# Spectral filter and gated feed-forward on one core: six batches sum their filter products ahead of a single inverse matmul, and a new calendar places the side work

## The chip, the cores and the metric

The kernel runs on one core of one Trainium2 chip. The metric is the device time of one execution in microseconds (us); lower is better. The times shown are of several executions of the same program; the profile is of one of them.

## The reference

The input x has 8 batches of 3008 rows by 256 columns. Each column of a batch goes through a real Fourier transform along its rows, is multiplied by a complex filter, and is transformed back. The result is normalized row by row and goes through a gated feed-forward layer.

```python
# _attn_ref
X = np.fft.rfft(x, axis=1)                    # x: 8 x 3008 x 256
F = (filt_r + 1j * filt_i)[None, :, :]
y = np.fft.irfft(X * F, n=x.shape[1], axis=1)
# _moe_ref, on y as 24064 x 256
rms = np.sqrt(np.mean(x * x, axis=-1, keepdims=True) + 1e-06)
xn = x / rms * rms_g
g = xn @ w_gate                               # 256 x 1536
silu = g * (1.0 / (1.0 + np.exp(-g)))
val = xn @ w_val
return (silu * val @ w_out).astype(np.float32)
```

## The kernel before

A transform of 3008 points is done as 64 times 47 points, in four matmul steps for each batch. Step A (`a_unit`, psum tile psa, L192) transforms over 64 points; the result goes to DRAM by `z_store` and comes back in another order by `t2_load`. Step B (`b_unit`, psb, L213) transforms over 47 points: of the 128 output partitions, the first 64 hold real parts and the last 64 imaginary parts. VectorE then multiplies the psum tile twice, by the real filter (L230, s1) and by the imaginary filter (L231, s2). The inverse of step B (`bi_unit`, psi, L239) is a sum of two matmuls per column of the grid, `wi[:, k, 0, :]` with s1 and `wi[:, k, 1, :]` with s2; the second table carries the swap of halves and the sign that a complex product needs. One unit handles two of the 32 grid columns, so a batch has 16 units and a unit has four inverse matmuls. ScalarE copies psi out (L244); `g_store` and `t4_load` go through DRAM again. The last step (`n_unit`, psn, L270) is the inverse over 64 points; ScalarE writes the scaled rows y (L275) and their squares sq (L277). `q_unit` sums the squares by eight very narrow matmuls (psq, L284), VectorE adds the epsilon (u, L288), GpSimd takes the power -1/2 (rho, L290), `rho_move` spreads it over partitions by way of DRAM (rb), and `xn_unit` multiplies on GpSimd (xn, L345).

The feed-forward layer is a list of 576 slots: 8 batches, 6 blocks of 512 rows (448 in the sixth), 12 blocks of 128 hidden columns. A slot issues `gv` (two matmuls each into pg and pv, L360; the Silu on ScalarE, L364; the product hh on VectorE, L365), then whatever the calendar `plan` has for the slot, then `down` for the slot two places earlier (four matmuls into po, L376). While the feed-forward layer of one batch runs, the transform of the next runs in its slots. Instructions go to the engines in the order in which they are written; nothing is moved later, and each engine works through its own list in order.

The order of the transform in the calendar, with t = 72 * (b - 1), is: a at t + 0 to 11, b every second slot from t + 16, the inverse three slots after its b, the n pairs from t + 57 every 8 slots, both halves in neighbouring slots. Batch 1 starts later and is packed closer. The first transform, of batch 0, runs before slot 0.

psum has eight banks: two each for pg and pv, two for po, and two named psM, which rotate over psa, psb, psi, psn and psq alike.

Of the kernel before, what the change touches and what calls it, by code (L numbers as in the profile page):

```python
# [38 lines left out]
def _make_tables():  # L39
    n2 = np.arange(N2)  # L40
    wa = np.zeros((P, P))
    wai = np.zeros((P, P))
    for h in range(2):
        for k2 in range(K2):
            c = np.cos(2 * np.pi * ((n2 * k2) % N2) / N2)
            s = np.sin(2 * np.pi * ((n2 * k2) % N2) / N2)
            r = slice(h * 64, h * 64 + 64)
            wa[r, h * 64 + k2] = c
            wai[h * 64 + k2, r] = c * (1.0 if k2 == 0 else 2.0)
            if k2 == 0:  # L50
                alt = 1.0 - 2.0 * (n2 % 2)
                wa[r, h * 64 + 32] = alt
                wai[h * 64 + 32, r] = alt
            else:
                wa[r, h * 64 + 32 + k2] = -s
                wai[h * 64 + 32 + k2, r] = -2.0 * s
    n1 = np.arange(N1)
    wb = np.zeros((KR, K2, P))
    wi = np.zeros((P, 1, 2, P))
    re, im = slice(0, N1), slice(SL, SL + N1)  # L60
    for k2 in range(K2):
        for s in range(48):

            if s < 24:
                k = k2 + 64 * s
                sign, q = 1.0, s
            else:
                j = s - 23
                k = 64 * j - (k2 if k2 else 32)
                sign, q = -1.0, 32 + s - 24  # L70
                if j == 24 and k2:
                    continue
            th = 2 * np.pi * ((n1 * k) % N) / N
            c, sn = np.cos(th), np.sin(th)
            if k == 0 or k == NF - 1:
                sn = np.zeros(N1)
            if k2:
                wb[re, k2, q] = c
                wb[im, k2, q] = sign * sn
                wb[re, k2, HALF + q] = -sn  # L80
                wb[im, k2, HALF + q] = sign * c
            else:
                src = re if s < 24 else im
                wb[src, k2, q] = c
                wb[src, k2, HALF + q] = -sn
                m = 1.0 if k in (0, NF - 1) else 2.0
                z = np.zeros(N1)
                g = (m * c, -m * sn)
                gr, gi = (g, (z, z)) if s < 24 else ((z, z), g)


                for qq, cols in ((re, 0), (im, 1)):
                    wi[q, 0, 0, qq] = (gr, gi)[cols][0]
                    wi[HALF + q, 0, 0, qq] = (gr, gi)[cols][1]
                    wi[q, 0, 1, qq] = (gr, gi)[cols][1]
                    wi[HALF + q, 0, 1, qq] = -(gr, gi)[cols][0]
    f = np.float16
    wi0 = wi[:, 0] * S_INV_B
    return wa.astype(f), (wai * S_INV_A).astype(f), wb.astype(f), wi0.astype(f), np.eye(P).astype(f)
# [3 lines left out]
def kernel(  # L103
# [27 lines left out]
    t1p = ctx.enter_context(tc.tile_pool(name="t1p", bufs=2))  # L131
    t2p = ctx.enter_context(tc.tile_pool(name="t2p", bufs=3))
    sp = ctx.enter_context(tc.tile_pool(name="sp", bufs=3))
    t3p = ctx.enter_context(tc.tile_pool(name="t3p", bufs=3))
    t4p = ctx.enter_context(tc.tile_pool(name="t4p", bufs=4))
    yp = ctx.enter_context(tc.tile_pool(name="yp", bufs=3))
    sqp = ctx.enter_context(tc.tile_pool(name="sqp", bufs=2))
# [5 lines left out]
    psG = ctx.enter_context(tc.tile_pool(name="psG", bufs=2, space=bass.MemoryType.PSUM))  # L143
    psV = ctx.enter_context(tc.tile_pool(name="psV", bufs=2, space=bass.MemoryType.PSUM))
    psO = ctx.enter_context(tc.tile_pool(name="psO", bufs=1, space=bass.MemoryType.PSUM))
    psM = ctx.enter_context(tc.tile_pool(name="psM", bufs=2, space=bass.MemoryType.PSUM))

    wa = glob.tile([P, P], FP16)
    wai = glob.tile([P, P], FP16)
# [28 lines left out]

    def bank(i, name):

        pool, tag = ((psM, "mx"), (psG, "pg"), (psV, "pv"))[i]
        return pool.tile([P, 512], FP32, tag=tag, name=name)

    def a_unit(b, i):
# [22 lines left out]
        st[b]["t2"][c] = t  # L207

    def b_unit(b, i):
        ps = bank(0 if b else i % 2, "psb").rearrange("p (a d) -> p a d", a=2)  # L210
        for u in range(2):
            k = 2 * i + u
            nc.tensor.matmul(ps[:, u, :], wb[:, k, :], st[b]["t2"][k // KC][:, k % KC, :],  # L213
                             start=True, stop=True)
        c, r = divmod(2 * i, KC)
        f1, f2 = fr[c][:, r:r + 2, :], fi[c][:, r:r + 2, :]
        if b:
            s1 = sp.tile([P, 2, D], FP16, tag="s1", name="s1")
            s2 = sp.tile([P, 2, D], FP16, tag="s2", name="s2")
        else:  # L220
            s1 = hp.tile([P, 512], FP16, tag="sg", name="sg").rearrange("p (a d) -> p a d", a=2)
            s2 = hhs[i % 4].rearrange("p (a d) -> p a d", a=2)
        eng = nc.vector
        if b == 0 and i % 2 and i > 4:
            eng = nc.gpsimd
            v = yp.tile([P, 2, 512], FP32, tag="y", name="v")
            v = v[:, 0, :].rearrange("p (a d) -> p a d", a=2)
            nc.scalar.activation(out=v, in_=ps, func=AXT.Copy)
            ps = v
        eng.tensor_tensor(out=s1, in0=ps, in1=f1, op=ALU.mult)  # L230
        eng.tensor_tensor(out=s2, in0=ps, in1=f2, op=ALU.mult)  # L231
        st[b]["s"][i] = (s1, s2)

    def bi_unit(b, i):
        s12 = st[b]["s"].pop(i)
        ps = bank(0 if b else 2, "psi").rearrange("p (a d) -> p a d", a=2)
        for u in range(2):
            for q in range(2):
                nc.tensor.matmul(ps[:, u, :], wi[:, 2 * i + u, q, :], s12[q][:, u, :],  # L239
                                 start=(q == 0), stop=(q == 1))  # L240
        c, r = divmod(i, 2)
        if r == 0:
            st[b]["t3"][c] = t3p.tile([KR, 4, D], FP16, tag="t3", name="t3")
        nc.scalar.activation(out=st[b]["t3"][c][:, 2 * r:2 * r + 2, :], in_=ps[0:KR], func=AXT.Copy)  # L244
# [18 lines left out]
    def n_unit(b, m, dh):  # L263
        if dh == 0:
            st[b]["y"][m] = yp.tile([P, 2, 512], FP32, tag="y", name="y")
        y = st[b]["y"][m]
        ps = psM.tile([P, 512], FP32, tag="mx", name="psn")
        for q in range(4):
            n1p = 4 * m + q
            nc.tensor.matmul(ps[:, ts(q, P)],  # L270
# [2 lines left out]
        if dh == 0:  # L273
            st[b]["sq"][m] = sqp.tile([P, 2, 512], FP16, tag="sq", name="sq")
        nc.scalar.activation(out=y[:, dh, :], in_=ps, func=AXT.Identity,  # L275
                             scale=gsb[:, dh:dh + 1])
        nc.scalar.activation(out=st[b]["sq"][m][:, dh, :], in_=ps, func=AXT.Square)  # L277

    def q_unit(b, m):
        sq = st[b]["sq"].pop(m)  # L280
        ps = psM.tile([P, 4], FP32, tag="mx", name="psq")
        for q in range(4):
            for dh in range(2):
                nc.tensor.matmul(ps[:, q:q + 1], sq[:, dh, ts(q, P)], ones,  # L284
# [7 lines left out]

    def rho_move(b, m):
        nc.sync.dma_start(r_d[b, m], st[b]["u"].pop(m))
        rb = rp.tile([P, P, 4], FP32, tag="rb", name="rb")
        nc.sync.dma_start(rb.rearrange("p a q -> p (a q)"),
                          r_d[b, m].rearrange("p q -> (p q)").partition_broadcast(P))
# [116 lines left out]

    def f_dup(c):
        nc.vector.tensor_copy(out=fr[c][HALF:P], in_=fr[c][0:HALF])
        nc.scalar.activation(out=fi[c][HALF:P], in_=fi[c][0:HALF], func=AXT.Copy)

    def wi_group(g):

# [3 lines left out]
            nc.tensor.matmul(ps[:, a, :], wb[:, 4 * g + a, :], ident[0:KR, :], start=True, stop=True)  # L424
        k = slice(4 * g + lo, 4 * g + 4)
        nc.scalar.activation(out=wi[:, k, 0, :], in_=ps[:, lo:4, :], func=AXT.Copy, scale=S_INV_B)
        for p0, sign in ((0, 1.0), (HALF, -1.0)):
            nc.vector.tensor_scalar(out=wi[p0:p0 + HALF, k, 1, :],
                                    in0=ps[HALF - p0:P - p0, lo:4, :], scalar1=sign * S_INV_B,
                                    scalar2=None, op0=ALU.mult)  # L430

    def gate(ap):
# [14 lines left out]
    with tc.manual_schedule():  # L447
# [58 lines left out]
        norm_first()  # L506
        w_load(1)
        w_load(2)
        n_unit(0, 1, 0)
        n_unit(0, 1, 1)  # L510
        for c in range(NXC):
            x_load(1, c)

# [1 line left out]
        plan = {}  # L515

        def at(slot, fn, *a):
            plan.setdefault(slot, []).append((fn, a))

        def norm_plan(b, m, s0):  # L520
            at(s0, n_unit, b, m, 0)
            at(s0 + 1, n_unit, b, m, 1)
            at(s0 + 3, q_unit, b, m)
            at(s0 + 5, rho_move, b, m)
            at(s0 + 10, xn_unit, b, m)

        at(1, q_unit, 0, 1)
        at(3, scale_split, 1)
        at(5, scale_apply, 1, 0)
        for m in range(2, 6):  # L530
            norm_plan(0, m, 2 + (m - 2) * 9)
        for b in range(1, B):
            t = (b - 1) * 72
            a0, b0, bs = (8, 24, 6) if b == 1 else (0, 16, 8)
            for i in range(12):
                at(t + a0 + i, a_unit, b, i)
                if i % 3 == 2:
                    at(t + a0 + i + 1, z_store, b, i // 3)
            for c in range(4):
                at(t + b0 - 3 + c if c < 3 else t + b0 + 8, t2_load, b, c)  # L540
            for i in range(16):
                s0 = t + b0 + bs * i // 4
                at(s0, b_unit, b, i)
                at(s0 + 3, bi_unit, b, i)
                if i % 2 == 1:
                    at(s0 + 4, g_store, b, i // 2)
            if b + 1 < B:
                for c in range(NXC):
                    at(t + 20 + 4 * c, x_load, b + 1, c)
            for c in range(4):  # L550
                at(t + 54, t4_load, b, c)
            for m in range(6):
                norm_plan(b, m, t + 57 + 8 * m)

        stores = {}
        for i in range(len(items) + 4):
# [40 lines left out]
```

## Time and profile before

| | |
|---|---|
| median of 8 runs | 991.09 us (988.02 to 994.0) |
| profiled execution: its time | 993.59 us |
| profiled execution: span of its instructions | 991.8 us |
| mean granted TensorE clock | 0.963 |
| TensorE busy | 911.2 us, 92% of the span |
| ScalarE busy | 606.3 us, 61% |
| VectorE busy | 594.1 us, 60% |
| GpSimd busy | 256.2 us, 26% |
| inverse matmuls of step B (psi) | 512, of which 384 belong to batches 2 to 7 |

Busy time is the time in which at least one instruction of the engine was under way. Matmuls overlap each other, so the length of one row is not what the matmul costs; the distance from its start to the start of the next one is. An engine's idle time matters where that engine, or what waits for it, ends last.

### The profile page before, as it was taken

To read this page: it belongs to the slowest core of one execution; us is meant where nothing else is said; L and a number is where in the kernel's file an instruction comes from. 1 tells how busy PE (TensorE), PEld (TensorE's weight loads), DVE (VectorE), ACT (ScalarE), POOL (GpSimd) and SP (SyncE) were. 2 spreads that over 40 slices of the span, in tenths; PEclk is the share of its full clock that TensorE was granted. 3 is DMA by queue.
4 is the path that set the end of the run, shared out by engine and by line. 5 is a ranking of instruction groups with operands and counts; after the bars stand their busy time and mean duration, and the time that the engine had idled before them with its cause. 6 is when DMAs were issued, how large, how long until landed. Compare 5 with 4: busy or idle time off the path is not lost.

```text
span 991.8 us, 17348 instructions
## 1 busy us (share of the span) xinstructions
PE 911.2 (92%) x6287; PEld 576.5 (58%) x6287; DVE 594.1 (60%) x961; ACT 606.3 (61%) x1061; POOL 256.2 (26%) x219
## 2 busy tenths in 40 slices
PE   3347989999999999999999999999999989999997
PEld 1224546665666566665666566665666556666654
DVE  6623468545775467655775468655775467655554
ACT  7343845576656865577656865577656756566543
POOL 3564231033301332032411323031411312024300
PEclk8567999999999999999999999999999999999999
DMA  8879473335623474324814375324734343322211
GB/s 191 141 138 168 111 155 79 106 99 116 152 75 97 104 174 98 102 78 125 163 51 126 88 154 125 108 63 110 164 81 125 88 111 90 99 70 62 43 43 40
DMA packets 94837, 106.98 MB, mean 108 GB/s; under 512 B 17112, under 2 KB 69464, under 8 KB 94560
## 3 DMA queue, kind: packets, MB, share of 16 engines
q1 hardware_dynamic: 85104, 87.92, 34.0%
q0 software_dynamic: 9552, 17.77, 12.0%
q8 instruction: 49, 0.80, 0.3%
q14 instruction: 36, 0.29, 0.1%
q10 hardware_dynamic: 96, 0.20, 0.1%
HBM read 70.62 MB, written 49.90 MB: 122 GB/s over the span
## 4 chain that ended last, share of the span: by engine, by line
PE 76%; DMA 9%; ACT 5%; issue 4%; DVE 3%; POOL 1%; SPq 1%; ACTq 0%; DVEq 0%; POOLq 0%
PE po L376 22%; PE pg L360 21%; PE pv L360 21%; PE psi L239 5%; DMA t<-z_tmp 3%; PE psb L213 3%; DMA fi<-in_filt_i_dram 2%; PE psn L270 2%; DMA g_tmp<-t 1%; DMA z_tmp<-t 1%; PE psa L192 1%; ACT sq L277 1%; ACT t L194 1%; DVE o L382 1%; DMA xc<-in_x_dram 1%
## 5 line engine op out<-in xcount | busy, mean ns | idle before, releaser
L365 DVE TENSOR_TENSOR hh<-pv,sg 128x512 f16<-128x512 f32 (+1 forms) x576 | 390.9, 679 | 333.0 <-ACT sg L364 210.5
L364 ACT ACTIVATE sg<-pg 128x512 f16<-128x512 f32 (+1 forms) x576 | 341.0, 592 | 295.8 <-PE pg L360 271.3
L376 PE MATMUL po<-wo,hh 128*128 128x256 f16 x2304 | 350.8, 273 | 3.5 <-DVE o L382 0.9
L360 PE MATMUL pg<-xn,wg 128*128 128x512 f16 (+1 forms) x1152 | 340.0, 377 | 0.0
L360 PE MATMUL pv<-xn,wv 128*128 128x512 f16 (+1 forms) x1152 | 339.8, 377 | 0.0
L376 PEld LDWEIGHTS <-hh 128*128 128x128 f16 x2304 | 221.3, 98 | 94.6 <-issue 16.4
L345 POOL TENSOR_TENSOR xn<-y,rb 128x1024 f16<-128x1024 f32 x46 | 132.1, 2873 | 315.5 <-DMA rb<-r_tmp 244.1
L360 PEld LDWEIGHTS <-wv 128*128 128x128 f16 x1152 | 113.2, 98 | 132.6 <-issue 3.0
L290 POOL TENSOR_TENSOR rho<-u,mhalf 128x4 f32<-128x4 f32 x48 | 48.7, 1014 | 328.9 <-DVE u L288 328.8
L360 PEld LDWEIGHTS <-wg 128*128 128x128 f16 x1152 | 113.2, 98 | 14.4 <-issue 0.6
L244 ACT ACTIVATE t<-psi 96x512 f16<-96x512 f32 x128 | 75.6, 593 | 32.3 <-PE psi L239 29.3
L239 PEld LDWEIGHTS <-wi 128*128 128x128 f16 x512 | 51.2, 102 | 55.7 <-issue 13.4
L230 DVE TENSOR_TENSOR s<-psb,fr 128x512 f16<-128x512 f32 x112 | 76.4, 682 | 10.0 <-PE psb L213 10.0
L231 DVE TENSOR_TENSOR s<-psb,fi 128x512 f16<-128x512 f32 x112 | 76.3, 681 | 0.0
L275 ACT ACTIVATE y<-psn,gsb 128x512 f32<-128x512 f32 x94 | 65.3, 695 | 10.2 <-PE psn L270 4.9
L213 PE MATMUL psb<-t,wb 96*128 96x256 f16 x256 | 52.4, 290 | 19.4 <-DMA t<-z_tmp 18.5
L239 PE MATMUL psi<-s,wi 128*128 128x256 f16 x448 | 67.3, 273 | 2.6 <-DVE s L231 2.6
L194 ACT ACTIVATE t<-psa 128x512 f16<-128x512 f32 x96 | 57.9, 615 | 5.7 <-PE psa L192 2.8
L277 ACT ACTIVATE sq<-psn 128x512 f16<-128x512 f32 x94 | 56.6, 603 | 0.0
L213 PEld LDWEIGHTS <-wb 96*128 96x128 f16 x256 | 25.1, 104 | 41.1 <-issue 18.3
L192 PE MATMUL psa<-xc,wa 128*128 128x512 f16 x96 | 37.2, 404 | 11.3 <-DMA xc<-in_x_dram 8.9
L270 PEld LDWEIGHTS <-t 128*128 128x128 f16 x376 | 29.4, 99 | 21.3 <-issue 0.6
(55 smaller groups left out, 329.8 us busy)
## 6 DMA issues: line engine op xcount, KB each, us to landing
out_dram<-o SPq DMA_DIRECT2D x88, 256.0 KB, 3.7
z_tmp<-t SPq DMA_DIRECT2D x128, 96.0 KB, 2.2
t<-z_tmp SPq DMA_DIRECT2D x32, 384.0 KB, 6.1
g_tmp<-t SPq DMA_DIRECT2D x64, 192.0 KB, 2.5
t<-g_tmp SPq DMA_DIRECT2D x126, 96.0 KB, 2.6
rb<-r_tmp SPq DMA_DIRECT2D x46, 256.0 KB, 4.1
xc<-in_x_dram POOLq DMA_DIRECT2D x56, 192.0 KB, 6.1
out_dram<-o SPq DMA_DIRECT2D x8, 192.0 KB, 3.0
```

The source lines that it names most:

```text
L194: nc.scalar.activation(out=dst, in_=src, func=AXT.Copy)
L213: nc.tensor.matmul(ps[:, u, :], wb[:, k, :], st[b]["t2"][k // KC][:, k % KC, :], start=True, stop=True)
L230: eng.tensor_tensor(out=s1, in0=ps, in1=f1, op=ALU.mult)
L231: eng.tensor_tensor(out=s2, in0=ps, in1=f2, op=ALU.mult)
L239: nc.tensor.matmul(ps[:, u, :], wi[:, 2 * i + u, q, :], s12[q][:, u, :], start=(q == 0), stop=(q == 1))
L244: nc.scalar.activation(out=st[b]["t3"][c][:, 2 * r:2 * r + 2, :], in_=ps[0:KR], func=AXT.Copy)
L277: nc.scalar.activation(out=st[b]["sq"][m][:, dh, :], in_=ps, func=AXT.Square)
L345: nc.gpsimd.tensor_tensor(out=xv, in0=yv, in1=rv.unsqueeze(1).to_broadcast([P, 2, 4, P]), op=ALU.mult)
L360: nc.tensor.matmul(ps[:, 0:w], wt[:, dt_, ts(jt, P)], xn[:, dt_, 0:w], start=(dt_ == 0), stop=(dt_ == 1))
L364: nc.scalar.activation(out=sg[:, 0:w], in_=pg[:, 0:w], func=AXT.Silu)
L365: nc.vector.tensor_tensor(out=hh[:, 0:w], in0=pv[:, 0:w], in1=sg[:, 0:w], op=ALU.mult)
L376: nc.tensor.matmul(po[s4 // 2][:, s4 % 2, :], hh[:, ts(s4, P)], wo[:, jt, :], start=(jt == 0 and s4 % 2 == 0), stop=(jt == JT - 1 and s4 % ...
```

## The change

For batches 2 to 7, s2 is formed with its halves exchanged: two VectorE products of 64 partitions each (`swap_unit`), reading one half of the psum tile and writing the other half of s2. GpSimd adds s1 and s2 to one tile s, and `bi_unit` does one matmul a column, with `wi[:, k, 0, :]` alone. The sign moves from the table to the copied half of the imaginary filter (`f_dup`, scale -1). Batches 0 and 1 keep two products and two inverse matmuls; in batch 1 every third unit has its products done on GpSimd, from a copy that ScalarE makes.

The two psM banks become one bank psM (psa, psi, psn) and one bank psB (psb, psq). The squares leave `n_unit` for a function of their own, `sq_unit`, which for batches from 1 on stands one slot later. `rho_move` is split in two, so that the load of rb has its own slot. `sq_unit` (from batch 1 on) and `swap_unit` are put at the head of their slot's list, which is still behind the slot's `gv`.

The calendar is new. For batches 3 to 7 a stands in slots that are 1 modulo 4, b and the inverse of two units earlier in slots 2 modulo 4, the first half product and n in slots 3 modulo 4, the second half product and the squares in slots 0 modulo 4, and q in slots 1 modulo 4. Batch 2 has the same grid for b and a lag of 4 slots from b to the inverse where the later batches have 8; its a steps stand in slots 22 to 44, among batch 1's b and inverse steps.

```diff
-                    wi[HALF + q, 0, 1, qq] = -(gr, gi)[cols][0]
+                    wi[HALF + q, 0, 1, qq] = (gr, gi)[cols][0]
...
+    ssp = ctx.enter_context(tc.tile_pool(name="ssp", bufs=3))
+    t3p = ctx.enter_context(tc.tile_pool(name="t3p", bufs=2))
...
-    psM = ctx.enter_context(tc.tile_pool(name="psM", bufs=2, space=bass.MemoryType.PSUM))
+    psM = ctx.enter_context(tc.tile_pool(name="psM", bufs=1, space=bass.MemoryType.PSUM))
+    psB = ctx.enter_context(tc.tile_pool(name="psB", bufs=1, space=bass.MemoryType.PSUM))
...
-        ps = bank(0 if b else i % 2, "psb").rearrange("p (a d) -> p a d", a=2)
+        ps = bank(3 if b else (0, 1, 3)[i % 3], "psb").rearrange("p (a d) -> p a d", a=2)
...
+            if b > 1:
+                nc.vector.tensor_tensor(out=s1, in0=ps, in1=f1, op=ALU.mult)
+                st[b]["s"][i] = (s1, s2, ps, f2)
+                return
...
-        if b == 0 and i % 2 and i > 4:
+        if (b == 0 and i % 2 and i > 4) or (b == 1 and i % 3 == 1):
...
+    def swap_unit(b, i, h):
+        s1, s2, ps, f2 = st[b]["s"][i]
+        a, e = slice(HALF * h, HALF * h + HALF), slice(HALF - HALF * h, P - HALF * h)
+        nc.vector.tensor_tensor(out=s2[a], in0=ps[e], in1=f2[e], op=ALU.mult)
+        if h:
+            s = ssp.tile([P, 2, D], FP16, tag="s", name="s")
+            nc.gpsimd.tensor_tensor(out=s, in0=s1, in1=s2, op=ALU.add)
+            st[b]["s"][i] = (s,)
...
+        n = len(ss)
         for u in range(2):
-            for q in range(2):
-                nc.tensor.matmul(ps[:, u, :], wi[:, 2 * i + u, q, :], s12[q][:, u, :],
-                                 start=(q == 0), stop=(q == 1))
+            for q in range(n):
+                nc.tensor.matmul(ps[:, u, :], wi[:, 2 * i + u, q, :], ss[q][:, u, :],
+                                 start=(q == 0), stop=(q == n - 1))
...
-        nc.scalar.activation(out=st[b]["sq"][m][:, dh, :], in_=ps, func=AXT.Square)
+        st[b]["sq"][m, dh] = ps
+
+    def sq_unit(b, m, dh):
+        nc.scalar.activation(out=st[b]["sq"][m][:, dh, :], in_=st[b]["sq"].pop((m, dh)),
+                             func=AXT.Square)
...
-        ps = psM.tile([P, 4], FP32, tag="mx", name="psq")
+        ps = psB.tile([P, 4], FP32, tag="mb", name="psq")
...
         def at(slot, fn, *a):
-            plan.setdefault(slot, []).append((fn, a))
+            todo = plan.setdefault(slot, [])
+            if fn in (sq_unit, swap_unit) and a[0]:
+                todo.insert(0, (fn, a))
+            else:
+                todo.append((fn, a))
...
+        def norm_plan(b, m, s0, s1, r):
+            for dh in range(2):
+                at((s0, s1)[dh], n_unit, b, m, dh)
+                at((s0, s1)[dh] + (b > 0), sq_unit, b, m, dh)
+            for d, fn in zip(r, (q_unit, rho_move, rho_load, xn_unit)):
+                at(s1 + d, fn, b, m)
...
         for m in range(2, 6):
-            norm_plan(0, m, 2 + (m - 2) * 9)
+            s0 = (2, 20, 28, 38)[m - 2]
+            norm_plan(0, m, s0, s0 + 2, (2, 3, 5, 8))
...
-            a0, b0, bs = (8, 24, 6) if b == 1 else (0, 16, 8)
+            if b == 1:
+                a_at = [8 + i for i in range(12)]
+                b_at = [24 + 3 * i // 2 for i in range(16)]
+                lag, t4_at, n_at = 3, 53, 55
+            elif b == 2:
+                a_at = [22 + 2 * i for i in range(12)]
+                b_at = [50 + 4 * i for i in range(16)]
+                lag, t4_at, n_at = 4, 118, 123
+            else:
+                a_at = [t - 103 + 12 * (i // 2) + 4 * (i % 2) for i in range(12)]
+                b_at = [t - 26 + 4 * i for i in range(16)]
+                lag, t4_at, n_at = 8, t + 46, t + 51
...
-                at(t + b0 - 3 + c if c < 3 else t + b0 + 8, t2_load, b, c)
+                at(b_at[0] - (4 if b > 2 else 3) + c if c < 3 else b_at[4] + 1, t2_load, b, c)
             for i in range(16):
-                s0 = t + b0 + bs * i // 4
+                s0 = b_at[i]
                 at(s0, b_unit, b, i)
-                at(s0 + 3, bi_unit, b, i)
+                if b > 1:
+                    at(s0 + 1, swap_unit, b, i, 0)
+                    at(s0 + 2, swap_unit, b, i, 1)
+                at(s0 + lag, bi_unit, b, i)
...
-                    at(t + 20 + 4 * c, x_load, b + 1, c)
+                    at(a_at[3 * c + 2] + 2, x_load, b + 1, c)
...
-                at(t + 54, t4_load, b, c)
+                at(t4_at + c, t4_load, b, c)
             for m in range(6):
-                norm_plan(b, m, t + 57 + 8 * m)
+                norm_plan(b, m, n_at + 8 * m, n_at + 8 * m + 4,
+                          (2, 4, 6, 10) if b > 1 else (2, 3, 4, 7))
```

More of the change, by code (lines that the diff above doesn't have):

```diff
@@ L133 @@
     sp = ctx.enter_context(tc.tile_pool(name="sp", bufs=3))
-    t3p = ctx.enter_context(tc.tile_pool(name="t3p", bufs=3))
+    ssp = ctx.enter_context(tc.tile_pool(name="ssp", bufs=3))
+    t3p = ctx.enter_context(tc.tile_pool(name="t3p", bufs=2))
     t4p = ctx.enter_context(tc.tile_pool(name="t4p", bufs=4))
@@ L179, in bank @@
     def bank(i, name):
-        pool, tag = ((psM, "mx"), (psG, "pg"), (psV, "pv"))[i]
+        pool, tag = ((psM, "mx"), (psG, "pg"), (psV, "pv"), (psB, "mb"))[i]
         return pool.tile([P, 512], FP32, tag=tag, name=name)
@@ L232, in b_unit @@
         st[b]["s"][i] = (s1, s2)
+    def swap_unit(b, i, h):
[6 more added lines that the diff above has]
+            st[b]["s"][i] = (s,)
     def bi_unit(b, i):
-        s12 = st[b]["s"].pop(i)
+        ss = st[b]["s"].pop(i)
         ps = bank(0 if b else 2, "psi").rearrange("p (a d) -> p a d", a=2)
+        n = len(ss)
         for u in range(2):
-            for q in range(2):
-                nc.tensor.matmul(ps[:, u, :], wi[:, 2 * i + u, q, :], s12[q][:, u, :],
-                                 start=(q == 0), stop=(q == 1))
+            for q in range(n):
+                nc.tensor.matmul(ps[:, u, :], wi[:, 2 * i + u, q, :], ss[q][:, u, :],
+                                 start=(q == 0), stop=(q == n - 1))
         c, r = divmod(i, 2)
@@ L266, in n_unit @@
         y = st[b]["y"][m]
-        ps = psM.tile([P, 512], FP32, tag="mx", name="psn")
+        ps = bank(0, "psn")
         for q in range(4):
@@ L294, in rho_move, with rho_load @@
         nc.sync.dma_start(r_d[b, m], st[b]["u"].pop(m))
+    def rho_load(b, m):
         rb = rp.tile([P, P, 4], FP32, tag="rb", name="rb")
@@ L416, in f_dup @@
         nc.vector.tensor_copy(out=fr[c][HALF:P], in_=fr[c][0:HALF])
-        nc.scalar.activation(out=fi[c][HALF:P], in_=fi[c][0:HALF], func=AXT.Copy)
+        nc.scalar.activation(out=fi[c][HALF:P], in_=fi[c][0:HALF], func=AXT.Copy, scale=-1.0)
     def wi_group(g):
@@ L426, in wi_group @@
         nc.scalar.activation(out=wi[:, k, 0, :], in_=ps[:, lo:4, :], func=AXT.Copy, scale=S_INV_B)
-        for p0, sign in ((0, 1.0), (HALF, -1.0)):
+        for p0 in (0, HALF):
             nc.vector.tensor_scalar(out=wi[p0:p0 + HALF, k, 1, :],
-                                    in0=ps[HALF - p0:P - p0, lo:4, :], scalar1=sign * S_INV_B,
+                                    in0=ps[HALF - p0:P - p0, lo:4, :], scalar1=S_INV_B,
                                     scalar2=None, op0=ALU.mult)
@@ L508 @@
         w_load(2)
-        n_unit(0, 1, 0)
-        n_unit(0, 1, 1)
+        for dh in range(2):
+            n_unit(0, 1, dh)
+            sq_unit(0, 1, dh)
         for c in range(NXC):
@@ L517, in at @@
         def at(slot, fn, *a):
-            plan.setdefault(slot, []).append((fn, a))
[L520 to L525, printed above, removed]
+            todo = plan.setdefault(slot, [])
[4 more added lines that the diff above has]
+        def norm_plan(b, m, s0, s1, r):
+            for dh in range(2):
+                at((s0, s1)[dh], n_unit, b, m, dh)
+                at((s0, s1)[dh] + (b > 0), sq_unit, b, m, dh)
+            for d, fn in zip(r, (q_unit, rho_move, rho_load, xn_unit)):
+                at(s1 + d, fn, b, m)
         at(1, q_unit, 0, 1)
@@ L535 @@
             for i in range(12):
-                at(t + a0 + i, a_unit, b, i)
+                at(a_at[i], a_unit, b, i)
                 if i % 3 == 2:
-                    at(t + a0 + i + 1, z_store, b, i // 3)
+                    at(a_at[i] + 1, z_store, b, i // 3)
             for c in range(4):
-                at(t + b0 - 3 + c if c < 3 else t + b0 + 8, t2_load, b, c)
+                at(b_at[0] - (4 if b > 2 else 3) + c if c < 3 else b_at[4] + 1, t2_load, b, c)
             for i in range(16):
-                s0 = t + b0 + bs * i // 4
+                s0 = b_at[i]
@@ L543 @@
                 at(s0, b_unit, b, i)
-                at(s0 + 3, bi_unit, b, i)
+                if b > 1:
+                    at(s0 + 1, swap_unit, b, i, 0)
+                    at(s0 + 2, swap_unit, b, i, 1)
+                at(s0 + lag, bi_unit, b, i)
                 if i % 2 == 1:
-                    at(s0 + 4, g_store, b, i // 2)
+                    at(s0 + lag + 1, g_store, b, i // 2)
             if b + 1 < B:
                 for c in range(NXC):
-                    at(t + 20 + 4 * c, x_load, b + 1, c)
+                    at(a_at[3 * c + 2] + 2, x_load, b + 1, c)
```

## Prediction

> **What bounds the kernel now.** I read the page first, then busy time by stretch, then the timeline of TensorE, then the other engines around one slot.
>
> ```profile
> PE   3347989999999999999999999999999989999997
> PEclk8567999999999999999999999999999999999999
> PE 76%; DMA 9%; ACT 5%; issue 4%; DVE 3%; POOL 1%; SPq 1%; ACTq 0%; DVEq 0%; POOLq 0%
> 500.00:525.00 25.00, 25.00 (x169) 16.24 (x167) 18.15 (x29) 14.46 (x25) 0.00 (x0) 1.00 0.33 83
> 550.00:575.00 25.00, 24.53 (x169) 14.53 (x168) 12.16 (x21) 20.44 (x37) 7.75 (x4) 1.00 0.43 112
> ```
>
> From slot 8 on (100 us) TensorE is busy nearly all the time, at full clock, and the chain that ended last lies on it for 76%. VectorE (18.15 us in the busier stretch) and ScalarE (20.44) have room. So matmul columns taken out, and waits of TensorE taken out or put in, are what counts.
>
> ```profile
> 566.39 0.39 PE L270 MATMUL psn<-wai,t 128*128 128x128 f16 x4
> 566.91 0.38 PE L192 MATMUL psa<-xc,wa 128*128 128x512 f16 x1
> 576.67 0.38 PE L213 MATMUL psb<-t,wb 96*128 96x256 f16 x2 [0.92 <-DMA t<-z_tmp]
> ...
> 581.03 0.59 PE L360 MATMUL pv<-xn,wv 128*128 128x512 f16 x2
> 581.46 0.60 PE L239 MATMUL psi<-s,wi 128*128 128x256 f16 x4
> 581.89 0.60 PE L376 MATMUL po<-wo,hh 128*128 128x256 f16 x4
> 582.33 0.59 PE L360 MATMUL pg<-xn,wg 128*128 128x512 f16 x2
> ```
>
> Read from start to start, an inverse unit of four matmuls costs 581.89 - 581.46 = 0.43 us, as po does; pg and pv 0.43 each, so a bare slot is 1.30. Psn, psa or psb cost 0.22, psq 0.20. The first two rows are 0.52 apart, not 0.22: psa waited 0.30 for a psum bank. Slots 72 to 503 (206.9 to 888.4 us) last 681.5 us; subtracting these contents (blocks of 448 rows cost 0.107 a slot less) leaves 25.4 us of waiting, some 3 to 6 a batch: psn and psa in one slot, the first psb behind its load, a VectorE copy of po in front of the products. Before slot 72 the same reading leaves 16.6, after slot 504 2.9.
>
> ```profile
> 478.82 0.39 PE L270 MATMUL psn<-wai,t 128*128 128x128 f16 x4
> 479.31 0.69 ACT L275 ACTIVATE y<-psn,gsb 128x512 f32<-128x512 f32 x1
> 479.89 0.59 ACT L277 ACTIVATE sq<-psn 128x512 f16<-128x512 f32 x1
> 484.01 0.59 PE L360 MATMUL pg<-xn,wg 128*128 128x512 f16 x2
> 484.64 0.60 ACT L364 ACTIVATE sg<-pg 128x512 f16<-128x512 f32 x1 [0.28 <-PE pg L360]
> 485.27 0.69 DVE L365 TENSOR_TENSOR hh<-pv,sg 128x512 f16<-128x512 f32 x1 [0.83 <-ACT sg L364]
> ...
> 22.50 5.63 DVE L428 TENSOR_SCALAR wi<-pst 64x512 f16<-64x512 f32 x8 [3.12 <-ACT wi L426]
> 29.48 0.69 DVE L230 TENSOR_TENSOR sg<-psb,fr 128x512 f16<-128x512 f32 x1 [0.21 <-PE psb L213]
> 30.09 0.68 DVE L231 TENSOR_TENSOR hh<-psb,fi 128x512 f16<-128x512 f32 x1
> L230 POOL TENSOR_TENSOR sg<-v,fr x6: 1252/1259/1280, 44.7 to 64.8; 128x512 f16<-128x512 f32 x6
> ```
>
> These are the clocks of a slot that starts at T: the Silu at T + 0.63, hh at T + 1.26. A psn bank is held from 478.82 to 480.48, 1.66 us. L428 is the nearest row to a half product, 64 partitions crossing halves: eight take 5.63, 0.70 each, where whole products follow each other after 0.60.
>
> **The change, part by part.**
>
> *Matmuls.* 6 batches x 16 units x half of 0.434 = **-20.8 us**, all in slots where TensorE has no slack.
>
> *Old waits, slots 72 to 503.* The calendar parts psn from psa, loads t2 four slots ahead of use instead of three and keeps the po copy (slots 1 modulo 12) away from the first product. I let 1.5 of the 25.4 us stay: **-23.9**. After slot 504, with the n halves apart: **-0.9**.
>
> *Steady ScalarE and psM, batches 3 to 7.* A slot has one extra activation beside the Silu, 0.59 + 0.70 at most, against slots of 1.30 to 1.74. With one bank psM: a starts at T + 0.87, its copy ends near T + 2.0, the inverse comes at T + 1.52 + 0.87 = 2.39; n comes after the inverse's copy with more room; sq runs from T + 1.13 to 1.73 of its slot, a comes at 1.30 + 0.87 = 2.17. Cost 0, covered by gaps of some 0.4 us; without them each would be paid for by TensorE directly, queued behind it po and the next slot.
>
> *VectorE and psB: q.* Nothing else on VectorE is late (4.8 us of work in four slots of 6.1), but psB is now alone. The second half product stands in slot 0 behind hh: hh from 1.26, 0.69 long, then 0.70, so it ends at 2.65 and the bank is free at about 2.70. q asks for the same bank in the next slot after pg and pv, at 1.30 + 0.87 = 2.17. TensorE waits 0.53 with po behind it. Counting the calendar, each of the 36 q of batches 1 to 6 follows such a half product: **+19.1** (15 if the half product starts 0.60 after hh and lasts 0.68; 0 if something delays q anyway).
>
> *GpSimd adds.* No row shows a sum of f16 tiles; the nearest, L230 on GpSimd at the same 128x512, is 1.26 us; half an xn row (2.87 for 1024) gives 1.44. I take 1.26. For batches 3 to 7 it has 8 slots, 12 us: free, even behind an xn and a rho (2.87 + 1.0); the x loads' issues on GpSimd, two of 0.56, fit too. For batch 2 the lag is 4 slots: the sum ends at 2.70 + 1.26 + 0.05 = 4.0 after its slot 0, the inverse comes at 1.30 + 0.87 + slot 1, which is 3.47 bare, 3.69 with a, over 4.1 with q. Four bare ones wait 0.51, six with a 0.29, six with q none: **+3.8** (6 with 1.44). The Trainium skill speaks against such an add (GPSIMD Engine Reference, Performance versus the Vector engine: about 2.6 cycles an element for two inputs, elementwise work belongs on VectorE); its rate gives an estimate of 1.11 us for 512 elements, which would make the term 2.3. I keep the row, which holds the fixed part too.
>
> *Slots 20 to 50.* Batch 2's a now meets batch 1's inverse and batch 0's n on the one psM bank, and here sq is in n's own slot. Slots 28, 30 and 40 have n, inverse, b, a: the inverse waits from 1.09 until 2.58 (bank held 1.66 + release), a another 0.6 for the inverse's copy: 2.1 each. Slot 38 (n, a) 1.5; 34, 36, 45 (inverse, a) and 42 (b behind q's u) 0.63 each; 32 (q behind b) 0.46: **10.8**. Before, slots 30 and 38 lost 1.09 and 0.75, and 12 to 14 0.35. The wait for the first t2 of batch 1 (3.71 us in the timeline, slot 24) is bound by its load; an n/a collision in slot 22 eats 1.5 of it, so about 2.3 remain. In the trace that 3.71 us gap was followed by pg and pv rows of 1.06 us, half clock, which with slots 25 and 26 cost 1.95 more. The Trainium skill (TensorE: Matmul & The Clock Gate, Part 1) has the clock fall after an idle window of about 3.4 us; by it 2.3 us keep the clock and the 1.95 goes, by the row alone it stays. I take half: 3.3 here against 6.0 before. Together 14.1 - 8.2 = **+5.9**.
>
> *DMA and queues.* No transfer is added. SP is the queue to watch: rho_move now waits there for a rho that stands behind an xn on GpSimd, about 3 us, with g_store and o_store behind it. g_store has 16 slots until its buffer is needed; t4 loads stand three slots behind the last g_store and five ahead of n: 0. Without that cover the 2.0 us of rho's landing would show before n. Start-up up to slot 8 waits for weights and for rho(0,1) in GpSimd's list, which is unchanged: 0; the second n(0,1), now waiting 1.7 us for the bank, hides in the wait of slot 5 (5.9 us).
>
> Sum: -20.8 - 23.9 - 0.9 + 19.1 + 3.8 + 5.9 = **-16.8**; the profiled execution's 993.59 becomes 976.8. It lay 2.5 above the median of 991.09, so the forecast is **974 us**, -1.7%.
>
> **The rivals.**
>
> *The q wait is not there* (slot 0 drawn out by something, or psB free sooner): 974 - 19 = 955. For it: a calendar with nothing in conflict would look so. Against it: the arithmetic rests on hh at T + 1.26, seen in every slot.
>
> *Half given back:* the same mechanisms with larger sizes: adds of 1.44, collisions in slots 20 to 50 that also delay xn (y buffers are shared with batch 1's copies), a late rb. Another 8 to 14 us: 982 to 988.
>
> *Slower: the single psM bank.* Place: a, inverse, n, squares of batches 2 to 7, once in every four slots. They have about 0.4 us to spare. If ScalarE ran its copies 0.6 us later than I read, each of 96 groups would lose 0.2 or more; 17 us, 0.18 a group, cancels the gain, and at 0.25 the time is 974 + 24 = 998. For it: with two banks psa already waits when n is in its slot. Against it: those were two n and two a in neighbouring slots.
>
> *It does not do what it says:* "at most one extra operation" fails in batch 1's stage, and is in the forecast as 10.8 us.
>
> **How the numbers follow.** The forecast 0.58 (966 to 981 by the bounds of q, add and clock), no q wait 0.12, half given back 0.16, slower 0.10, and 0.04 that losses just cancel. A measurement here tells 0.3%, about 3 us, from no change. Faster: 0.58 + 0.12 + 0.16 = 0.86; same 0.04; slower 0.10. The range leaves out the slower and the cancelled cases and the lower half of the case without q waits: 956 to 987.
>
> **What would show it.** psi rows fall from 512 to 320. A bare q slot of 1.51 lasts 2.0, with psq waiting on VectorE's half product, some 36 times. psi of batch 2 waits on GpSimd in ten units, later batches never. Slots 28, 30, 40 last over 4 us. Half products 0.68 to 0.70 and adds near 1.26. Steady stretches hold no other wait of TensorE. I am wrong if a stretch from 350 to 850 us shows TensorE waiting for ScalarE on psM, or no wait before psq.

## The result: 8 us instead of 17

The changed kernel takes 982.86 us (median of 11 runs, 980.46 to 986.01) against 991.11 (32 runs): a ratio of 0.9916, 95% interval 0.9901 to 0.9932. Forecast was 974, a gain of 17; measured is a gain of 8.25. The direction was right and the range held the time; the size was off by half. The profiled execution took 985.8 us with a span of 983.7, so the spans fell by 8.1 us, as the medians did.

The page of the changed kernel, the rows of TensorE's load, granted clock and the chain that ended last, and the same two stretches as before:

```profile
PE   3356978999999999999999999999999999999997
PEclk8556999999999999999999999999999999999999
PE 72%; DVE 8%; DMA 7%; issue 5%; ACT 4%; POOL 3%; SPq 0%; DVEq 0%; POOLq 0%; ACTq 0%
```

```profile
500.00:525.00 25.00, 24.87 (x156) 14.98 (x154) 17.60 (x27) 14.68 (x25) 6.54 (x6) 1.00 0.68 148
550.00:575.00 25.00, 24.20 (x180) 15.48 (x179) 19.37 (x33) 18.70 (x32) 13.32 (x11) 1.00 0.41 91
```

TensorE is still the bound, but VectorE has gone from 3% to 8% of the chain: something on VectorE now ends a wait of TensorE. No stretch looks overloaded; VectorE's 19.37 of 25 us would never suggest it. The waits of TensorE name it. First the kernel before, slots 72 to 503, then the changed kernel, the same slots (us in total, times, longest):

```profile
PE psb L213 <- DMA t<-z_tmp: 9.0, 6, 2.8
```

```profile
PE psq L304 <- DVE s L243: 13.8, 34, 0.4
PE psi L255 <- POOL s L246: 1.9, 5, 0.5
```

The wait for step B's loads is gone. In its place stand 34 waits of psq for the half product (two more stand before slot 72, 36 in all), and some of the inverse for the GpSimd sum. The view counts an idle stretch from the modelled end of the last row, so it shows 0.4 us of each; from start to start it is 0.57. One of them, in the timeline of the changed kernel (start, length):

```profile
572.33 0.69 DVE L243 TENSOR_TENSOR s<-psb,fi 64x512 f16<-64x512 f32 x1
573.13 0.69 DVE L387 TENSOR_TENSOR hh<-pv,sg 128x512 f16<-128x512 f32 x1
573.60 0.59 PE L382 MATMUL pv<-xn,wv 128*128 128x512 f16 x2
573.85 0.68 DVE L243 TENSOR_TENSOR s<-psb,fi 64x512 f16<-64x512 f32 x1
574.60 0.35 PE L304 MATMUL psq<-ones,sq 128*128 128x1 f16 x8 [0.40 <-DVE s L243]
574.71 1.15 POOL L246 TENSOR_TENSOR s<-s,s 128x512 f16<-128x512 f16 x1 [4.92 <-DVE s L243]
```

pv is through at 574.03 (573.60 + 0.43) and psq is next in TensorE's list. The second half product ends at 574.53, psq starts at 574.60. This is the wait that the forecast drew, at the place it named; it cost 0.57 instead of 0.53.

### The profile page after: what moved, and what is told of

Its sections match the earlier page's. It is cut to its first block, busy times and chain, and to the rows that moved or that the text cites. A ratio compares the mean times of both kernels' runs of the same rounds, so it can differ in the third digit from the quotient of the medians.

```text
span 983.7 us, 17361 instructions
## 1 busy us (share of the span) xinstructions
PE 894.0 (91%) x6095; PEld 554.4 (56%) x6095; DVE 670.5 (68%) x1047; ACT 633.5 (64%) x1066; POOL 376.9 (38%) x325
## 4 chain that ended last, share of the span: by engine, by line
PE 72%; DVE 8%; DMA 7%; issue 5%; ACT 4%; POOL 3%; SPq 0%; DVEq 0%; POOLq 0%; ACTq 0%
PE po L398 22%; PE pg L382 21%; PE pv L382 19%; DVE hh L387 4%; DVE s L243 3%; PE psi L255 3%; ACT sg L386 3%; PE psb L215 2%; PE psn L286 2%; PE psa L194 2%; DMA fi<-in_filt_i_dram 2%; DMA g_tmp<-t 2%; PE psq L304 1%; DMA z_tmp<-t 1%; DVE o L404 1%
## 5 line engine op out<-in xcount | busy, mean ns | idle before, releaser
L246 POOL TENSOR_TENSOR s<-s,s 128x512 f16<-128x512 f16 x96 | 110.6, 1152 | 375.4 <-DVE s L243 338.5
L243 DVE TENSOR_TENSOR s<-psb,fi 64x512 f16<-64x512 f32 x192 | 132.2, 689 | 5.9
L255 PEld LDWEIGHTS <-wi 128*128 128x128 f16 x320 | 33.5, 106 | 59.7 <-issue 25.4
L223 DVE TENSOR_TENSOR s<-psb,fr 128x512 f16<-128x512 f32 x96 | 65.5, 682 | 0.7 <-PE psb L215 0.2
L255 PE MATMUL psi<-s,wi 128*128 128x256 f16 x256 | 46.7, 275 | 6.9 <-ACT sq L296 3.9
```

The costliest lines, as they stand in the source:

```text
L223: nc.vector.tensor_tensor(out=s1, in0=ps, in1=f1, op=ALU.mult)
L243: nc.vector.tensor_tensor(out=s2[a], in0=ps[e], in1=f2[e], op=ALU.mult)
L246: nc.gpsimd.tensor_tensor(out=s, in0=s1, in1=s2, op=ALU.add)
L255: nc.tensor.matmul(ps[:, u, :], wi[:, 2 * i + u, q, :], ss[q][:, u, :], start=(q == 0), stop=(q == n - 1))
```

## The experiments

All medians in this section are compared within one session, with its own runs of the kernel before: 994.39 in the first four, 991.2 in the next four, 989.39 in the last two. Lost time in a slot is always read from start to start of TensorE's rows, less 0.217 us for each matmul of 512 columns and in proportion.

**The changed kernel again.** No edit.

> The changed kernel as it is, for comparison on the same chip and to see which waits come back in a second profile. Theory A (all waits follow from the calendar): 983 us, 36 waits of 0.57 us before psq, 2.1 us lost in slots 28, 30 and 40, the pair of half-clock rows near slot 31 again, and about 2 us in slot 18. Theory B (slots 18 and 31 are accidents of one execution): the same time within 3 us, but those two waits are gone or elsewhere.

981.71 us, a ratio of 0.9871 (0.9847 to 0.9894). The 36 psq waits and the losses of slots 28, 30 and 40 (2.13, 2.05, 2.05) are the same to 0.1 us; slot 18 lost 1.7. The half-clock rows of slot 31 (1.6 us in the first profile) are not there. So theory A holds for all but the clock, which differs between executions. The two sessions' ratios differ by more than their intervals allow, mainly through the kernel before; I use the sessions' own references.

**psq behind po.** `q_unit` of batches 1 to 7 is called after `down` in its slot.

```diff
+            late = []
             for fn, a in plan.get(i, ()):
-                fn(*a)
+                if fn is q_unit and a[0]:
+                    late.append(a)
+                else:
+                    fn(*a)
...
+            for a in late:
+                q_unit(*a)
```

> The eight narrow psq matmuls of batches 1 to 7 are issued behind the slot's four po matmuls instead of in front of them; nothing else changes. Theory A (psq waits 0.57 us for the bank that the second half product still reads, 36 times): po fills 0.43 us of that wait, a psa another 0.22, so the time falls by 17 to 20 us, to about 964. Theory B (the wait only moves, to the next slot's b or to po for want of hh): it falls by less than 6 us.

969.82 us, 11.9 less than the changed kernel (0.9751, 0.9726 to 0.9775, against 0.9871). A slot with a step A, in its timeline:

```profile
563.34 0.69 DVE L243 TENSOR_TENSOR s<-psb,fi 64x512 f16<-64x512 f32 x1
563.52 0.38 PE L194 MATMUL psa<-xc,wa 128*128 128x512 f16 x1
563.74 0.60 PE L398 MATMUL po<-wo,hh 128*128 128x256 f16 x4
564.17 0.34 PE L304 MATMUL psq<-ones,sq 128*128 128x1 f16 x8
```

psa follows pv at once, po follows psa, and psq finds the bank free. Of 20.7 us lost in front of psq 2.2 remain; some 2 come back at batch 2's inverse, which a late psq had covered, and 1.2 at the next slot's psb, which now waits 0.12 ten times. The profiled spans of this run and of the changed kernel's second profile differ by 14.7, the medians by 11.9, both short of the 17 to 20 that theory A named. Its cause holds (the bank, and what can stand in front of psq), its size does not; the move takes nothing from po, which does not need what psq needs.

**Other banks in slots 22 to 49.** Batch 2's step A takes its psum from the pv banks, batch 1's inverse from the pg banks.

```diff
-        ps = bank(0 if b else i % 3, "psa")
+        ps = bank((2 if b == 2 else 0) if b else i % 3, "psa")
...
-        ps = bank(0 if b else 2, "psi")
+        ps = bank((1 if b == 1 else 0) if b else 2, "psi")
```

> Step A of batch 2 takes its psum tile from the pv banks and the inverse of batch 1 from the pg banks, so that in slots 22 to 49 only n uses psM. Theory A (the waits of slots 22 to 45 are collisions on the single psM bank): slots 28, 30 and 40 fall from 4.5 to about 2.4 us and slots 34, 36, 45 lose their 0.63; 8 to 11 us less, and with them the half clock of slot 31. Slot 22 gives its 1.4 us to the wait for the load in slot 24. Theory B (ScalarE, with up to four activations in such a slot, is the limit there): pg and pv now wait for the copies instead, and under 4 us are won.

974.86 us, 6.9 less (0.9804, 0.9777 to 0.9832). Slots 28 to 49 lose 2.1 us instead of 10.6 to 12.1. The timelines of slot 30 in the changed kernel and of slot 28 here:

```profile
144.15 0.39 PE L286 MATMUL psn<-wai,t 128*128 128x128 f16 x4
145.16 0.59 ACT L296 ACTIVATE sq<-psn 128x512 f16<-128x512 f32 x1
145.80 0.60 PE L255 MATMUL psi<-s,wi 128*128 128x256 f16 x4 [1.26 <-ACT sq L296]
147.08 0.38 PE L194 MATMUL psa<-xc,wa 128*128 128x512 f16 x1 [0.46 <-ACT t L260]
```

```profile
137.03 0.39 PE L286 MATMUL psn<-wai,t 128*128 128x128 f16 x4
137.26 0.60 PE L255 MATMUL psi<-s,wi 128*128 128x256 f16 x4
137.69 0.38 PE L215 MATMUL psb<-t,wb 96*128 96x256 f16 x2
137.92 0.38 PE L194 MATMUL psa<-xc,wa 128*128 128x512 f16 x1
```

Above, the inverse starts 1.65 us after psn because one bank is read by y and sq first; below, 0.23 after. ScalarE has the same activations and is not the limit. Slots 18 to 20 lost 2 us more than in the changed kernel in this profile, 1.7 of it in rows at half clock behind the wait of slot 18, so not all of the 8.5 to 10 us arrived; the medians' 6.9 lies under the 8 to 11 of theory A, whose cause the timeline shows.

**Two products and two inverse matmuls, new calendar.** The half products and the sum are left out.

```diff
-        nc.vector.tensor_tensor(out=s2[a], in0=ps[e], in1=f2[e], op=ALU.mult)
-        if h:
-            s = ssp.tile([P, 2, D], FP16, tag="s", name="s")
-            nc.gpsimd.tensor_tensor(out=s, in0=s1, in1=s2, op=ALU.add)
-            st[b]["s"][i] = (s,)
+        nc.vector.tensor_tensor(out=s2, in0=ps, in1=f2, op=ALU.mult)
+        st[b]["s"][i] = (s1, s2)
...
-                    at(s0 + 2, swap_unit, b, i, 1)
```

> The calendar, banks and lags of the changed kernel, but batches 2 to 7 form two whole products as before (the second one a slot after the first), no sum, and two inverse matmuls a column. It puts back 20.8 us of matmul and takes away the GpSimd sums and one of three VectorE operations. Theory A (the sum's gain was eaten by the waits that it brought: psB held a slot longer in front of q, 20.7 us, and batch 2's inverse behind the sum, 4.7 us): 983 + 20.8 - 25.4 = 978, no slower than the changed kernel, with no wait before psq. Theory B (q waits for another reason, the calendar's): 983 + 20.8 = 1004, q waits stay.

973.91 us, 7.8 less than the changed kernel although it does all the matmuls of the kernel before (0.9802, 0.9775 to 0.9829). In slots 72 to 503 TensorE waits for next to nothing: 0.8 us by the starts. Its page:

```profile
PE 900.0 (93%) x6287; PEld 574.3 (59%) x6287; DVE 594.9 (61%) x951; ACT 633.2 (65%) x1066; POOL 269.1 (28%) x229
PE 85%; DMA 8%; ACT 2%; issue 2%; DVE 1%; POOL 1%; SPq 0%; DVEq 0%; ACTq 0%; POOLq 0%
```

The second product is done one slot after b, so psB is free before psq asks. This is the verdict on the change: **the calendar, with its two single banks and batch 1's products on GpSimd, is worth some 20 us without the sum (2.0%), and the sum, which takes 20.8 us of matmul away, cost 8 on top of it**. The changed kernel loses what this one does not: 20.7 us before psq, 4.7 at batch 2's inverse and some 3 where po waits for the copy of its second bank, 28 in all.

**Later slots for batch 2's x loads.**

```diff
-                    at(a_at[3 * c + 2] + 2, x_load, b + 1, c)
+                    at((18, 23, 29, 35)[c] if b == 1 else a_at[3 * c + 2] + 2, x_load, b + 1, c)
```

> The changed kernel with the four loads of batch 2's x at slots 18, 23, 29 and 35 instead of 12, 15, 18 and 21; step A of batch 2 still starts in slot 22. Theory A (these loads, pulled forward by the new calendar, slow the landing of batch 1's z stores, whose median there rose from 2.7 to 4.2 us and whose longest from 3.4 to 7.5, so that a step A buffer comes free late in slot 18): the 1.7 to 2.1 us of slot 18 go and slot 24 waits less; 2 to 4 us less in all. Theory B (the stores land late for another reason, such as the weights still arriving): slot 18 keeps its wait. A risk: x(2,0) could arrive late for slot 22.

981.11 us (0.9903, 0.9884 to 0.9921); slot 18 still lost 1.95. But the edit had moved only half of what it meant to. Each load is two transfers; the four of the first two loads went out together as in the changed kernel, before slot 18 begins at 113.1 us:

```profile
106.98 2.17 POOL L178 DMA_DIRECT2D xc<-in_x_dram  x4
```

GpSimd had nothing in front of them, and nothing else ties its list to a slot. The other four went out at 132.7 us instead of 113 to 120, and slot 24 lost 1.0 us instead of 2.4, as it does in every run below that moves them; in the six profiles of this calendar that do not, it lost 1.4 to 2.7. So slot 18 is undecided here and tried again below.

**A lag of 8 slots for batch 2.**

```diff
-                lag, t4_at, n_at = 4, 118, 123
+                lag, t4_at, n_at = 8, 122, 127
```

> The changed kernel with a lag of 8 slots for batch 2's inverse, its t4 loads and n four slots later. Theory A (batch 2's inverse waits for the GpSimd sum, 4.7 us in ten units): these waits go, 4 to 5 us less. Theory B (n of batch 2 four slots later now holds up xn of its first block at slot 144): a new wait there of 1 to 5 us takes the gain back.

978.62 us (0.9875, 0.9855 to 0.9895), 2.5 less than the run beside it. The waits of batch 2's inverse are gone (slots 72 to 117 lose 2.4 us, all in front of psq, instead of 5.8), and no wait for xn appears. That is less than the 4 to 5 of theory A. Slots 28 to 30 lost 1.7 more in this profile, again with half-clock rows; whether the other executions have them, and so what the medians miss, is not shown.

**All four edits.** The four diffs above in one kernel.

> All four edits on the changed kernel together: psq behind po, other banks for batch 2's step A and batch 1's inverse, later x loads, lag 8 for batch 2. With the first two of these measured at -11.9 and -6.9 us, 2 to 4 and 4 to 5 us for the others, and some 2 us that the lag saves once psq no longer covers it: 982 - 28 = 954. If the waits were not additive (a wait removed only shows the next): 960 to 965.

953.10 us (0.9608, 0.9584 to 0.9631), 28.0 less than the run with later slots, where 954 was expected. That it came so close is in part luck: the sum counted 2 to 4 us for the x loads and 4 to 5 for the lag, and the medians of the single runs add up to some 21, not 28. Read from start to start, the waits do add up. Between slots 8 and 503 the four edits alone took some 14, 8.5, 1 and 3.6 us out of the 46 that the changed kernel loses in its second profile, and together they take 30; the rest, 2 us, is batch 2's inverse, which came back when psq alone was moved.

**All four edits, two products.** The same with the edit of the two products.

> The same four edits, but with two whole products and two inverse matmuls for batches 2 to 7, no sum: it differs from the run with all four edits by the sum alone. If the sum is worth its matmuls once nothing waits for it, that run is faster than this one by 20.8 us less 1 to 3, and this one, by its own terms, is at 974 - 7 - 3 = 964 where no lag or psq waits are left to remove, which puts the other below 947. If the time of that run is 954 as its own terms say, the sum is worth about 10. If VectorE's third operation or the GpSimd sums cost something more, under 5.

964.52 us (0.9740, 0.9717 to 0.9764). With batch 2's inverse no longer waiting and psq hardly, the sum is worth 11.4 us of its 20.8. In slots 118 to 503 that run waits 7.4 us and this one 0.7: with shorter slots po waits for the VectorE copy of its bank (0.29 twice a batch), psq still waits 0.13 where no step A stands in its slot, the psb behind it 0.09 to 0.15, and xn is late once. The remaining 2 to 3 us are not placed in the medians. In the two profiles little is missing: slot 8 begins at 101.5 us there and at 97.4 here, though the two programs are alike up to that slot, which in the twelve profiles begins between 96.8 and 101.5.

**Batch 2's x loads behind a gate.** Three of the four chunks follow a one-element GpSimd copy that reads the first t2 of batch 1.

```diff
+        def x_gated(c):
+            if c == 1:
+                gate(st[1]["t2"][0][0:1, 0, 0:1])
+            x_load(2, c)
...
-                    at(a_at[3 * c + 2] + 2, x_load, b + 1, c)
+                    if b == 1 and c:
+                        at(24, x_gated, c)
+                    else:
+                        at(a_at[3 * c + 2] + 2, x_load, b + 1, c)
```

> In the run with later slots for batch 2's x loads the loads were issued at 107 us all the same: a slot orders a DMA only against GpSimd's own list, and the rho of batch 0 that used to stand in front of them now comes later. Here three of the four chunks stand behind a one-element GpSimd copy that waits for the first t2 of batch 1, with the rest as in the changed kernel. Theory A (these loads slow the z stores of batch 1, which land after up to 7.5 us): the z stores land within 4 us, the 1.6 to 2.1 us of slot 18 go, and 2 to 4 us are won in all, 978 to 980. Theory B (the stores are slow for another reason): slot 18 keeps its wait, and the time is 982.

978.44 us (0.9891, 0.9873 to 0.9908; no run of the ungated kernel stands beside it, so its gain is read in the trace). Slots 8 to 21 lose 0.2 us instead of 2.1; slot 24 loses 1.0, as it did with the later slots. In the changed kernel ScalarE's copy of step A waited for the buffer that a z store still read, and TensorE behind it (first fence, its timeline). The other three show the four stores of that buffer, issued between 107 and 110 us: how long ScalarE's copy waited for them, and their shortest, median and longest time to landing. They are of the changed kernel, the run with later slots and this one:

```profile
116.64 0.60 ACT L196 ACTIVATE t<-psa 128x512 f16<-128x512 f32 x1 [2.58 <-DMA z_tmp<-t]
117.29 0.38 PE L194 MATMUL psa<-xc,wa 128*128 128x512 f16 x1 [1.91 <-ACT t L196]
```

```profile
  ACT t L196: 2.6, 1
DMA to landing us min/median/max: 3.4/5.3/6.6
```

```profile
  ACT t L196: 2.5, 1
DMA to landing us min/median/max: 3.4/5.4/6.4
```

```profile
  ACT t L196: 0.7, 1
DMA to landing us min/median/max: 3.5/4.9/5.1
```

In the kernel before the longest of these four took 3.4. Theory A, and narrower than it was put: the run with later slots and this one differ in this stretch by the second load, which went out at 108 us there and at 127 here. A load that the new calendar pulled forward slowed the stores beside it.

**All edits with the gate.** The diff just shown replaces the later slots.

> The run with all four edits, with the gate in place of the later slots. Theory A: 953 - 2 to 4, so 949 to 951. Theory B: 953. A risk for both: x(2,1) lands after slot 28 asks for it.

951.74 us (0.9614, 0.9597 to 0.9632), 3.9% faster than before. Against all four edits with the later slots (953.10, 0.9608) nothing can be told apart. In the profile slots 8 to 27 lose 1.4 instead of 2.8 us, but slot 33 loses 2.1 that the other run does not lose:

```profile
141.52 2.86 POOL L367 TENSOR_TENSOR xn<-y,rb 128x1024 f16<-128x1024 f32 x1 [6.44 <-DMA rb<-r_tmp]
145.66 0.27 PE L255 MATMUL psi<-s,wi 128*128 128x256 f16 x1 [0.82 <-POOL s L236]
146.88 0.49 PE L255 MATMUL psi<-s,wi 128*128 128x256 f16 x3 [0.95 <-POOL s L237]
```

Batch 1's inverse waits for products that stand in GpSimd's list behind an xn, which waits for rb. The load of rb took 9.7 us to land here and 6.8 in the other run; the gated x loads went out around it, at 128 to 135 us. That they slowed it is likely and not shown by a run.

## Why the prediction was half right

The sum of the forecast, and what the first profile of the changed kernel shows in place of each term (us; negative is a gain):

| term | forecast | measured |
|---|---|---|
| half of the inverse matmuls (psi 512 to 320) | -20.8 | -20.9 |
| old waits, slots 72 to 503 | -23.9 | -22.0 |
| after slot 504 | -0.9 | -0.6 |
| psq behind the half product, 36 times | +19.1 | +20.7 |
| batch 2's inverse behind the sum | +3.8 | +4.7 |
| slots 8 to 49 | +5.9 | +11.1 |
| start-up to slot 8 | 0 | -1.0 |
| sum | -16.8 | -8.0 |

*What held.* The mechanism of the likeliest case: 36 waits at psq, none at psM in steady slots, batch 2 alone waiting for the sum, slots 28, 30 and 40 at 4.5 us. Two edits that take away the first and the last of these give 12 and 7 us. Against the rivals: the psq wait was there, and a psM wait in steady slots was not. The time itself lies outside the 966 to 981 of that case, where the rival "half given back" put it, 982 to 988: the same mechanisms with larger sizes, though by x loads and clock rather than by the larger adds, late xn and late rb that it named.

*What failed: the term of slots 20 to 50.* Of the 8.8 us between the two sums 5.2 lie here, +11.1 measured against +5.9, for three reasons. First, a slip in the working: the wait for the first t2 was shortened by the 1.5 us lost in slot 22, but those 1.5 us were then not counted (slot 22 lost 1.42). Second, the queue step. The text said that no transfer is added and looked at SP; it did not follow the x loads of batch 2, which the diff moves from slots 20 to 32 to slots 12 to 21, nor the rho of block 3, which moved from slot 14 to slot 24 and had held them back on GpSimd (the kernel before, then the changed one):

```profile
112.60 1.01 POOL L290 TENSOR_TENSOR rho<-u,mhalf 128x4 f32<-128x4 f32 x1 [6.96 <-DVE u L288]
113.56 1.14 POOL L176 DMA_DIRECT2D xc<-in_x_dram  x2
```

```profile
108.11 2.17 POOL L178 DMA_DIRECT2D xc<-in_x_dram  x4
```

They went out at 108 us beside batch 1's z stores, and the slowest of the four stores that slot 18 waits for took 6.6 us instead of 3.4: slot 18, 2.1 us, shown by the gate. Third, the clock. The forecast took half of 1.95 us for slots 25 and 26 and nothing elsewhere; 1.4 were lost in slot 25 and 1.6 in slot 31. In the second profile of the changed kernel neither was, and slots 8 to 49 are at +7.3 against the kernel before, so some 4 of the 5 us change from one execution to the next. The rule of the Trainium skill that I weighed there (TensorE: Matmul & The Clock Gate, Part 1, an idle window of about 3.4 us) did not decide it: the clock fell after a wait of 2.36 us, and after two slots with several short ones.

*Small sizes.* The half product starts 0.72 us after hh, not 0.69, and psq 0.07 after its end: 0.57 a wait, 1.6 us in all. The sum takes 1.15 us, nearer to the estimate of 1.11 from the Trainium skill's rate (GPSIMD Engine Reference, Performance versus the Vector engine) than to the row that I took (1.26), but it starts 0.17 us after the half product, not 0.05: 0.9 us more. Of the old waits 3.4 us stayed, not 1.5: in twelve of the slots 2 modulo 12 po waits up to 0.29 for the copy of its bank.

*What the forecast did not ask.* It added a gain of 20.8 to a cost of 19.1 + 3.8 that the same edit brings and did not set them against each other. The comparison with two products under the new calendar stood in its own numbers, -20.8 + 19.1 + 3.8 = +2.1; the runs give +8.

## What to carry to other kernels

When an engine is full, the time of a slot is set by who asks for a buffer first after whom, not by busy shares: write for each single buffer when its last reader ends and when the next writer asks. Before a cheap instruction is made to wait in the list of the full engine, see whether longer work that needs nothing of it can stand in front; here psq behind po was worth more than half of all the matmuls saved. And where a calendar moves several things at once, run its parts alone: here the sum in the title cost 8 us as it was placed and was worth 11 once hardly anything waited for it.

## What the hardware showed that was not expected

TensorE fell to half clock after less idleness than I had assumed. In the changed kernel, right after slot 30:

```profile
147.29 0.74 PE L398 MATMUL po<-wo,hh 128*128 128x256 f16 x4
147.83 1.06 PE L382 MATMUL pg<-xn,wg 128*128 128x512 f16 x2
148.68 1.06 PE L382 MATMUL pv<-xn,wv 128*128 128x512 f16 x2
149.54 1.06 PE L255 MATMUL psi<-s,wi 128*128 128x256 f16 x4
```

The rows take 1.06 us instead of 0.59, and the longest idle stretch in front of them is 1.26. Between 148 and 150.5 us the granted clock is 0.50. In the second profile of the same kernel, with the same waits, it did not happen. Waits of 2.36 and 2.69 us in slot 24 were followed by the same, waits of 1.0 to 2.0 there were not. In slot 18 a wait of 2.13 us was followed by it (in the run with other banks), waits of 2.07 and 2.09 were not. What exactly triggers it stays open.

A slot number in a calendar does not hold back a DMA: it only orders it within the list of the engine that issues it. In the run with later slots GpSimd, with nothing in front, issued from 107 us on what was written for slots 18 and 23; slot 18 began at 113.1.
